# Decode-attention backward on one core: five of 128 stores cut into pieces on two queues instead of one

## The chip, the cores and the metric

The kernel runs on one NeuronCore of a Trainium2 chip. The metric is the device time of one execution in microseconds (us). The engines are named as the profile names them: PE (TensorE, matrix multiply), DVE (VectorE), ACT (ScalarE), POOL (GpSimd) and SP (SyncE, which only issues transfers here). PEld is the weight load of PE. Three engines issue DMA transfers, each on a queue of its own: SP on q1, ACT on q10, POOL on q0. The transfers of all three are carried by the same 16 DMA engines of the core.

## The reference

The kernel computes softmax attention for a single query row and its gradients, for 64 heads (2 batches of 32), 8192 keys, head dimension 128, all in bf16:

```
scores = q . k^T / sqrt(128);  p = softmax(scores);  out = p . v
inputs:  q, grad_out [2,32,1,128];  k, v [2,32,8192,128]
returns: out, dq [2,32,1,128];  dk, dv [2,32,8192,128]
```

With one query row, `dv` of a head is the outer product of `p` with `grad_out`, and `dk` that of the scores' gradient with `q`. So each head reads 2 MB of keys and 2 MB of values, and writes 2 MB of `dk` and 2 MB of `dv`: 512 MB (of 2^20 bytes) in all, which is 537 of the 539 MB (of 10^6 bytes) on the profile's page.

## The kernel before, in words

**Tiling.** The keys of a head are one tile `kt` of 128 partitions x 16 KB: partition p holds tokens 64p to 64p+63, one contiguous row of 16 KB in memory. The values are a tile `vt` of the same shape. There are five buffers of each (`UNITS = 5`). Per head, PE turns the tile blockwise (line 115), ACT copies the result out of PSUM (line 122), PE forms scores and products, DVE finishes the softmax, and DVE overwrites `vt` with `dv` and `kt` with `dk` in place (`outer`, line 288). From there the tiles are stored.

**Order.** The work is written out by hand, with no reordering within an engine (`manual_schedule`, lines 377 to 443). The loop runs over heads h = 0 to 64, in eight steps j. Step j of turn h turns an eighth of head h and finishes head p = h - 1. In step 3 of turn h the `dv` of head p is stored, in step 7 its `dk`; they are called value store p and key store p below. At the end of turn h, SP issues `load(h + 3)`: first the keys, then the values. A load needs a free buffer: the keys of head p + 5 normally wait for key store p to land, the values of p + 5 for value store p (SP, line 106). SP and ACT both go through their instructions strictly in order; so does POOL.

**Landing semaphores.** A transfer that is issued raises a semaphore when it has landed. The program has eight of them for the transfers of SP and ACT together, and eight more for POOL's. They are dealt out in turn, along one order of all transfers which the planner (the Tile layer) makes when the kernel is built. An instruction that is to issue a transfer first waits until the transfer that had the same semaphore before has landed. The planner's order around a head p, read off the semaphore numbers of the program: keys p + 4, values p + 4, value store p, key store p, and so on.

**The stores.** `store(h, w)` (line 345) sends a tile off as a single transfer from ACT (line 348), 128 rows of 16 KB, for 123 of the 128 tiles; the last head's two tiles go in halves. The five tiles with `(2h + w) % 26 == 12` go through `store_by_fifteen` (line 306) instead. These are the `dv` tiles of heads 6, 19, 32, 45 and 58. There POOL sends a tile off in 24 transfers (`rows`, line 316), made of every fourth row, or of two rows 32 apart. Between these stand 11 transfers `turn(n)` (line 302): each copies 2n pieces of 4 bytes into the tile `spare`, whose contents nobody reads. Each row of a `rows` transfer of size 8192 moves as two pieces of 8 KB, one of size 16384 in one piece. Rows 16 to 19 and 48 to 51 (`fifth`), eight of 128, are sent two at a time and by themselves.

Of the kernel before, what the change touches and what calls it, by code (L numbers as in the profile page):

```python
# [18 lines left out]
RARE = 26  # L19
# [4 lines left out]
def kernel(  # L24
# [11 lines left out]
    nc = tc.nc  # L36
# [40 lines left out]
    dk_v = out_2.rearrange("b h (p n) d -> (b h) p n d", n=NT)  # L77
    dv_v = out_3.rearrange("b h (p n) d -> (b h) p n d", n=NT)
# [17 lines left out]
    heads = [Head() for _ in range(BH)]  # L96
# [200 lines left out]
    def turn(n):  # L297

        i = 4 * len(turns)
        turns.append(n)  # L300
        two = lambda t: t.rearrange("p (a b) -> p a b", a=2)
        nc.gpsimd.dma_start(  # L302
            out=two(spare[0:n, :])[:, :, i : i + 2], in_=two(q_rows[0:n, :])[:, :, 0:2]
        )

    def store_by_fifteen(h, w):

        dst, src = (dv_v, dk_v)[w][h], heads[h].kv[1 - w]

        def rows(lo, n, step=4, size=8192):
            own = slice(lo, lo + step * (n - 1) + 1, step)
            nc.gpsimd.dma_start(out=dst[own], in_=src[own], max_dma_last_dim=size)  # L316

        def fifth(r):
            rows(16 + r, 2, step=32)

        for r in range(4):

            if r == 1:
                fifth(r)
                turn(14)
            rows(52 + r, 11)
            rows(r, 4, size=16384)
            if r == 0:
                fifth(r)
                turn(3)  # L330
            elif r == 3:
                turn(10)
                fifth(r)
                turn(9)
            else:
                turn(5)
            rows(20 + r, 3)
            if r == 2:
                fifth(r)
                turn(14)  # L340
            rows(96 + r, 8)
            rows(32 + r, 4, size=16384)
            turn(5)

    def store(h, w, a=0, b=NT):
        if (2 * h + w) % RARE == RARE // 2 - 1:
            return store_by_fifteen(h, w)
        nc.scalar.dma_start(out=(dv_v, dk_v)[w][h][:, a:b, :], in_=heads[h].kv[1 - w][:, a:b, :])
# [16 lines left out]
    for i in range(2):  # L365
# [3 lines left out]
            out=qz[i][:, 0 : 4 * BH].rearrange("p (h z) -> p h z", z=4)[:, :, 3], in_=tps[:]  # L369
# [7 lines left out]
    with tc.manual_schedule():  # L377
# [59 lines left out]
        for w, dst in enumerate((o_rows, dq_rows)):  # L437
            tps = ps_tp.tile([BH, P], BF16, name="tps", tag="tp")
            nc.tensor.transpose(tps[:], colsT[:, w, :], ident_bf[:])  # L439
            rows = const.tile([BH, D], BF16, name=f"rows{w}")  # L440
# [33 lines left out]
```

## Time and profile before

| | us |
|---|---|
| median of 3 runs | 1276.52 (1276.35 to 1276.57) |
| the profiled execution | 1276.51 |
| its span, first to last instruction | 1274.4 |

| engine | busy us | share of the span |
|---|---|---|
| PE | 1060.1 | 83% |
| DVE | 892.3 | 70% |
| ACT | 961.0 | 75% |
| POOL | 104.5 | 8% |

The page also has rows for DMA: the mean busy share of the 16 DMA engines and the bytes per second in 40 slices of the span, the share of each queue, and for each kind of issue the median time from issue to landing: 21.4 us for a load of keys, 30.6 us for one of values, 24.9 and 22.5 us for stores from ACT. The first piece of each of the five tiles is issued at 138.63, 389.08, 648.81, 905.30 and 1164.06 us.

How to read it: a timeline row gives start, length, engine, line, operation, `out<-in`, and in brackets how long the engine sat idle before and what ended that. A letter q behind an engine's name means its sequencer: it issues or waits, and the engine computes nothing. Each turn of the loop issues two loads (SP, line 106) and two stores (ACT, line 348).

### The profile page before, as it was taken

How to read it: one execution, taken by the hardware profiler on the slowest of the kernel's cores; microseconds unless marked ns; L12 is line 12 of the kernel's file. 1: busy time of each engine (PE TensorE's matmuls, PEld its weight loads, DVE VectorE, ACT ScalarE, POOL GpSimd, SP SyncE). 2: the span in 40 equal slices, each digit the busy share in tenths (PEclk: the TensorE clock that was granted, in tenths of full speed). 3: DMA queues.
4: the chain of work that ended last, by engine and by line, in shares of the span. 5: the costliest groups of instructions: out<-in, count | busy, mean ns of one | idle time of the engine just before them, and what ended most of it. 6: DMA issues, size and time to landing. Idle time of an engine off the chain costs nothing. (4 is left out here: it accounts for less than half of the span.)

```text
span 1274.4 us, 31597 instructions
## 1 busy us (share of the span) xinstructions
PE 1060.1 (83%) x13444; PEld 708.9 (56%) x13444; DVE 892.3 (70%) x1576; ACT 961.0 (75%) x1107; POOL 104.5 (8%) x189
## 2 busy tenths in 40 slices
PE   5999889849998798399996984999969849999694
PEld 4666566526665565266664652666546526666462
DVE  1888858728887487288884863888856738888486
ACT  5888778739887687289875873988848838888583
POOL 1000211000002110000021200000212000001220
PEclk9999989969999799699997996999989979999797
DMA  9999999999999999999999999999999999999998
GB/s 394 419 429 426 428 426 427 426 431 429 427 428 426 425 426 427 426 422 427 428 426 423 424 426 425 422 426 429 425 418 427 428 428 415 429 427 428 424 425 345
DMA packets 43837, 539.00 MB, mean 423 GB/s; under 512 B 10192, under 2 KB 10192, under 8 KB 10192
## 3 DMA queue, kind: packets, MB, share of 16 engines
q1 hardware_dynamic: 18432, 268.44, 49.7%
q10 hardware_dynamic: 18320, 258.02, 47.7%
q0 software_dynamic: 6944, 10.51, 2.2%
q8 instruction: 105, 1.72, 0.5%
q14 instruction: 36, 0.29, 0.1%
HBM read 268.47 MB, written 268.47 MB: 421 GB/s over the span
## 5 line engine op out<-in xcount | busy, mean ns | idle before, releaser
L122 ACT CAST ev<-tp 128x1024 bf16<-128x1024 f32 x960 | 933.3, 1017 | 290.0 <-PE tp L115 141.2
L115 PE MATMUL tp<-ident_bf,vt 128*128 128x128 bf16 x4096 | 328.9, 226 | 132.3 <-ACT ev L122 117.2
L115 PEld LDWEIGHTS <-vt 128*128 128x128 bf16 x4096 | 266.7, 102 | 210.3 <-issue 185.0
L115 PE MATMUL tp<-ident_bf,kt 128*128 128x128 bf16 x4096 | 318.7, 221 | 8.8 <-DMA kt<-in_k_dram 7.2
L115 PEld LDWEIGHTS <-kt 128*128 128x128 bf16 x4096 | 238.9, 98 | 135.7 <-issue 124.5
L288 DVE TENSOR_TENSOR vt<-qd,P 128x2048 bf16<-128x2048 bf16 x256 | 306.6, 1219 | 0.2 <-DVE rawsb L142 0.2
L288 DVE TENSOR_TENSOR kt<-qd,dS 128x2048 bf16<-128x2048 bf16 x256 | 306.1, 1217 | 0.0
L131 PE MATMUL raw<-ev,qz 128*4 128x512 bf16 x2048 | 202.3, 384 | 0.3 <-ACT ev L122 0.3
L142 DVE COPY rawsb<-raw 128x512 f32<-128x512 f32 x128 | 88.6, 692 | 132.9 <-PE raw L131 130.5
L316 POOL DMA_DIRECT2D out_dram<-vt x120 | 67.0, 560 | 1018.5 <-DVE vt L288 822.4
L174 DVE TENSOR_REDUCE mp<-turned 128x1 f32<-128x64 f32 x64 | 14.1, 221 | 131.0 <-PE turned L148 130.2
L256 PE MATMUL acc<-vt,wz 128*32 128x512 bf16 x1024 | 102.1, 389 | 0.0
L256 PE MATMUL acc<-kt,wz 128*32 128x512 bf16 x1024 | 100.9, 387 | 0.9 <-DVE wz L203 0.9
L148 PE MATMUL turned<-ident_f,rawsb 128*128 128x128 f32 x512 | 87.4, 296 | 11.6 <-DVE rawsb L142 9.8
L120 DVE CAST ev<-tp 128x1024 bf16<-128x1024 f32 x64 | 78.4, 1225 | 16.7 <-PE tp L115 16.7
L131 PEld LDWEIGHTS <-qz 128*4 128x4 bf16 x2048 | 46.5, 81 | 55.3 <-issue 3.9
L148 PEld LDWEIGHTS turned<-ident_f,rawsb 128*128 128x128 f32 x512 | 57.1, 147 | 29.5 <-DVE rawsb L142 29.3
L256 PEld LDWEIGHTS <-wz 128*32 128x32 bf16 x2048 | 52.4, 93 | 29.2 <-DVE wz L203 1.6
L180 DVE TENSOR_REDUCE gm<-misc 1x1 f32<-1x128 f32 x64 | 17.8, 279 | 45.2 <-PE misc L178 45.2
L200 PEld LDWEIGHTS misc<-ld,ones_f 128*128 128x128 f32 x256 | 38.4, 189 | 15.3 <-DVE ld L227 15.3
L200 PE MATMUL misc<-ld,ones_f 128*128 128x1 f32 x256 | 45.9, 248 | 0.7 <-DVE ld L227 0.6
L302 POOL DMA_DIRECT2D spare<-in_q_dram x57 | 34.2, 600 | 123.0 <-DMA out_dram<-vt 107.8
(45 smaller groups left out, 332.7 us busy)
## 6 DMA issues: line engine op xcount, KB each, us to landing
kt<-in_k_dram SPq DMA_DIRECT2D x64, 2048.0 KB, 21.4
vt<-in_v_dram SPq DMA_DIRECT2D x64, 2048.0 KB, 30.6
out_dram<-kt ACTq DMA_DIRECT2D x63, 2048.0 KB, 24.9
out_dram<-vt ACTq DMA_DIRECT2D x58, 2048.0 KB, 22.5
out_dram<-vt POOLq DMA_DIRECT2D x20, 176.0 KB, 22.6
out_dram<-vt POOLq DMA_DIRECT2D x40, 64.0 KB, 22.8
out_dram<-vt POOLq DMA_DIRECT2D x20, 128.0 KB, 22.5
out_dram<-vt ACTq DMA_DIRECT2D x2, 1024.0 KB, 8.6
```

Source lines behind the costliest of these rows:

```text
L115: nc.tensor.matmul(tp[:, i, :], lhsT=x.kv[w][:, n, :], rhs=ident_bf[:], start=True, stop=True)
L120: nc.vector.tensor_copy(out=ev[:], in_=tp[:])
L122: nc.scalar.copy(out=ev[:], in_=tp[:])
L131: nc.tensor.matmul(raw[32 * k : 32 * k + 4, :], lhsT=qz[w][:, at : at + 4], rhs=evs[k // 2][:, 4 * (k % 2) : 4 * (k % 2) + 4, :].rearrange ...
L142: nc.vector.tensor_copy(out=x.raw[:], in_=raw[:])
L148: nc.tensor.transpose(out[:, i], x.raw[:, i * P : (i + 1) * P], ident_f[:])
L180: nc.vector.reduce_max(out=x.gm[:], in_=mT, axis=AX.X)
L200: nc.tensor.matmul(x.lsum, lhsT=ones_f[:], rhs=x.ld[:, w : w + 1], start=True, stop=True)
L256: nc.tensor.matmul(acc[32 * g : 32 * g + 32, :], lhsT=wz[w][:, n // 4, at : at + 32], rhs=rows[:, n : n + 4, :].rearrange("p n d -> p (n d)"),
L288: nc.vector.tensor_tensor(out=x.kv[1 - w][:, n : n + CH, :].rearrange("p n (d t) -> p n d t", t=2), in0=row.unsqueeze(1).to_broadcast([P, ...
L302: nc.gpsimd.dma_start(out=two(spare[0:n, :])[:, :, i : i + 2], in_=two(q_rows[0:n, :])[:, :, 0:2])
L316: nc.gpsimd.dma_start(out=dst[own], in_=src[own], max_dma_last_dim=size)
```

## The change

`store_by_fifteen` alone is changed. ACT now sends eight transfers of four rows each at its start: rows lo, lo + 4, lo + 8, lo + 12 for lo = 0 to 3 and 32 to 35. They stand in ACT's instruction stream where, for any other tile, the one store stands. POOL sends the other 96 rows: 20 + r, three rows, and 96 + r, eight rows, for r = 0 to 3; rows 16 to 19 as one transfer and rows 48 to 51 as another; and rows 52 to 95 as one transfer of 44 rows. That makes 11 transfers of POOL's with rows, and 9 turns (7 for the second and the fourth of the five tiles, where `odd` is 1) instead of 24 and 11. Over the five stores POOL's transfers go from 175 to 96, and ACT gets 40 more. All rows of POOL's move as two pieces of 8 KB; ACT's rows are not cut.

```
+        odd = ((2 * h + w) // RARE) % 2
-        def rows(lo, n, step=4, size=8192):
+        def rows(lo, n, step=4):
             own = slice(lo, lo + step * (n - 1) + 1, step)
-            nc.gpsimd.dma_start(out=dst[own], in_=src[own], max_dma_last_dim=size)
-
-        def fifth(r):
-            rows(16 + r, 2, step=32)
-
+            nc.gpsimd.dma_start(out=dst[own], in_=src[own], max_dma_last_dim=8192)
+
+        for lo in (0, 1, 2, 3, 32, 33, 34, 35):
+            nc.scalar.dma_start(out=dst[lo : lo + 13 : 4], in_=src[lo : lo + 13 : 4])
         for r in range(4):
-            if r == 1:
-                fifth(r)
-                turn(14)
-            rows(52 + r, 11)
-            rows(r, 4, size=16384)
+            if r == 2 and odd:
+                rows(48, 4, 1)
+                turn(12)
+            rows(20 + r, 3)
             if r == 0:
-                fifth(r)
-                turn(3)
-            elif r == 3:
-                turn(10)
-                fifth(r)
-                turn(9)
-            else:
-                turn(5)
-            rows(20 + r, 3)
-            if r == 2:
-                fifth(r)
-                turn(14)
+                if odd:
+                    rows(16, 4, 1)
+                    turn(12)
+                else:
+                    turn(4)
+                    rows(16, 4, 1)
+                    turn(8)
+            if r == 2 and not odd:
+                turn(8)
+                rows(48, 4, 1)
+                turn(4)
             rows(96 + r, 8)
-            rows(32 + r, 4, size=16384)
             turn(5)
+        rows(52, 44, 1)
+        turn(5)
```

## The prediction

> **What bounds the kernel now.** I read the DMA rows of the page first, then SP's waits, then the timelines of POOL and ACT around one of the five stores, then stages by window.
>
> ```profile
> DMA  9999999999999999999999999999999999999998
> GB/s 394 419 429 426 428 426 427 426 431 429 427 428 426 425 426 427 426 422 427 428 426 423 424 426 425 422 426 429 425 418 427 428 428 415 429 427 428 424 425 345
> ...
> q1 hardware_dynamic: 18432, 268.44, 49.7%
> q10 hardware_dynamic: 18320, 258.02, 47.7%
> q0 software_dynamic: 6944, 10.51, 2.2%
> ```
>
> The 16 DMA engines are busy in every slice at some 427 GB/s, while PE is busy 83% and ACT 75%. So bytes are the bound: what the DMA engines lose is lost, and what a compute engine loses can be made up. The loads, q1, take 49.7% of 16 x 1274.4 us for 128 transfers: 10134 / 16 / 128 = 4.95 us for one 2 MB transfer that has all engines to itself, twice that beside a store.
>
> ```profile
> SPq L106 <- DMA out_dram<-kt: 906.1, 59, 39.0
> SPq L106 <- DMA out_dram<-vt: 206.3, 21, 11.4
> ```
>
> SP's queue stands still nearly all the time until a store lands. So the loads are as far ahead as the five buffers let them be: when stores stop being issued, loads stop as soon as the buffers are full.
>
> ```profile
> 138.63 1.67 POOL L316 DMA_DIRECT2D out_dram<-vt  x3 [133.92 <-DVE vt L288]
> 140.30 0.58 POOL L302 DMA_DIRECT2D spare<-in_q_dram  x1
> 140.88 1.68 POOL L316 DMA_DIRECT2D out_dram<-vt  x3
> 142.55 0.62 POOL L302 DMA_DIRECT2D spare<-in_q_dram  x1
> 147.37 0.56 POOL L316 DMA_DIRECT2D out_dram<-vt  x1 [4.20 <-DMA out_dram<-vt]
> 149.20 0.57 POOL L302 DMA_DIRECT2D spare<-in_q_dram  x1 [1.27 <-DMA out_dram<-vt]
> ```
>
> This is a store by pieces: eight transfers back to back, then the ninth waits 4.20 us for the first to land, and so on. That is what eight landing semaphores dealt in turn look like. POOL does nothing else, so its wait costs nothing. ACT has other work, and the same rule. SP's timeline, the load's time to landing among the DMA issues, and ACT's timeline:
>
> ```profile
> 397.93 0.33 SPq L106 DMA_DIRECT2D kt<-in_k_dram  x1
> ```
>
> ```profile
> kt<-in_k_dram SPq DMA_DIRECT2D x1, 2048.0 KB, 20.5
> ```
>
> ```profile
> 403.31 3.90 ACT L122 CAST ev<-tp 128x1024 bf16<-128x1024 f32 x4 [0.56 <-PE tp L115]
> 418.54 0.34 ACTq L348 DMA_DIRECT2D out_dram<-vt  x1
> 418.97 1.93 ACT L122 CAST ev<-tp 128x1024 bf16<-128x1024 f32 x2 [11.77 <-issue]
> ```
>
> Here value store 20 is the eighth transfer after the load of keys 22 (issued 397.93, landed 20.5 us later, at 418.4). ACT stands from 407.2 until 418.5, issues, and only then copies on: 11.77 us idle, with PE behind it. A store of ACT's thus waits for a load of SP's that shares its semaphore. In the stage around it the DMA engines stay full:
>
> ```profile
> core 0: us, PE busy (x) PEld busy (x) DVE busy (x) ACT busy (x) POOL busy (x), PEclk, DMA share, GB/s
> ...
> 400.00:418.00 18.00, 8.39 (x114) 5.22 (x111) 10.12 (x15) 6.53 (x7) 3.87 (x7) 0.81 1.01 427
> ...
> 1205.00:1240.00 35.00, 33.57 (x440) 22.29 (x437) 29.50 (x53) 31.39 (x37) 6.79 (x13) 1.00 1.01 424
> 1240.00:1252.00 12.00, 11.33 (x153) 7.43 (x149) 10.73 (x18) 10.35 (x14) 2.46 (x5) 1.00 0.94 395
> ```
>
> The two columns that matter are ACT busy and, last but one, DMA share (1.01: full). So a short stop of ACT is free. The 1205 to 1240 row shows compute at its own pace (PE 96% busy): ACT issues stores at 1202.54, 1210.91, 1219.02, 1227.39, 1235.49, 1243.84 and 1251.96, 8.24 us apart or 16.5 us a head. DMA needs 4 x 4.95 = 19.8 us a head.
>
> **The change, part by part.** The sum is made against the profiled execution, 1276.51 us (span 1274.4 and 2.1 around it); the median, 1276.52, is the same.
>
> *Fewer transfers of POOL's.* q0's 2.2% is 449 engine-us; its 10.51 MB at q1's price (10134 engine-us for 268.44 MB) are 397. The other 52, 3.3 us per DMA engine, are turns and landing marks of 177 transfers. 79 go: -1.5 us. Ends: 0 and -3.3. POOL's issue time (0.56 us each) hides behind its waits.
>
> *Other places for eight rows, one transfer of 44 rows.* No view tells which DMA engine carries a row. Bounds: the engines are full until 1240 and 0.94 busy to 1252, so a better balance can give 0.06 x 12 = 0.7 us; one row more per store on one engine costs 5 x 4.95 / 8 = 3 us. I take 0, having no row for either side.
>
> *Eight issues on ACT.* 8 x 0.34 us instead of no issue: 2.7 us of ACT per store, hidden in waits like the 11.77 us one. Without that cover it would be 13.6 us over five stores.
>
> *What these eight wait for.* Eight transfers in a row take all eight landing semaphores, so each of the last eight transfers of SP and ACT in the planner's order must have landed before ACT goes on. In that order value store p follows the loads of keys and values p + 4; the pieces stand in its place. So the eighth piece waits for values p + 4. Behind it on ACT are the copies out of PSUM, so PE (two buffers) and then DVE stop too, and key store p, which frees the buffer that keys p + 5 need. Keys and values p + 4 need stores p - 1, already issued. So ACT waits for the last loads that can be issued at all, until all five buffers are full and q10 is empty. Queued behind key store p are SP's loads of p + 5. POOL's pieces do not wait for ACT.
>
> Followed through the second store (p = 19, all up to 389.1 as before): value store 18 lands at 372.48 + 35.5 = 408.0, key store 18 at 380.61 + 37.7 = 418.3; then q10 is empty. Keys 22 land at 418.4. Values 22 (before: 398.36 + 30.7 = 429.1, beside stores) now need 4.95 alone: 423.4. Keys 23 (issued 418.41 on the landing of key store 18): 428.3. Values 23: 433.3. ACT stands from 389.1 to 433.3, 44 us. Key store 19 comes one half-head later, 8.2, and its first packet about 1 us after the issue (an estimate: SP's first load is issued at 0.74, and the trace's first packet of its queue starts at 1.74): 442.5. So 9.2 us without load or store. Key store 19 then runs alone, and keys 24 follow its landing another 1.1 us late. From there each store sets off a load, 9.9 us of DMA for every 8.24 of compute: full again. Hole: 10.3 us, less what is left of POOL's pieces, of which the last is the 44-row transfer: eight pieces of 8 KB for each of 11 engines, at 4.95 / 16 = 0.31 us each, 2.5 us. I take 8 us a store. Ends: 4 (much more of POOL's work left over) and 11 (none, and a later key store). The 44 us themselves compute makes up in 13 heads: 13 x (19.8 - 16.5) = 43.
>
> The first, third and fourth store have the same order of loads: 4 x 8 = 32 us (16 to 44).
>
> *The fifth store* has only five heads behind it. Without shift: key store 57 lands at 1155.59 + 35.0 = 1190.6, keys 61 at 1170.70 + 21.1 = 1191.8; values 61, keys 62, values 62 alone: 3 x 4.95, so 1206.6. Key store 58 at 1214.8, key store 62 four heads (65.9) later: 1280.7, against 1251.96 now. What follows is 12.8 us to the last key store's issue (1264.79) as now, and its landing, 8.0 us now behind three halves in the queue, 4 to 5 alone. So the end comes 28.7 - 3.5 = 25 us later (20 to 28).
>
> Sum: 1276.5 - 1.5 + 0 + 32 + 25 = 1332. From the ends: 1276.5 - 3.3 - 0.7 + 16 + 20 = 1308.5 and 1276.5 + 3 + 44 + 28 = 1351.5; not all at once, so 1311 to 1347.
>
> **The rivals.**
>
> *Keys, not values.* If the planner puts the values' load behind the first piece, where POOL's first piece now stands in its order, the last wait is for keys p + 4. Then values p + 4, 4.95 us, fill half of the hole: 3 us a store, and the end 20 us late: 1276.5 - 1.5 + 12 + 20 = 1307 (1296 to 1315). Against it: a store of ACT's is placed behind the copies of its step, later than POOL's piece.
>
> *No hole; not slower.* ScalarE's wait is hidden like the one at 407. It decides at 9.2 us before the loads run out: were ACT free by 433.3 - 9.2 = 424.1, after 35 us, no gap would open, as loads fill q1 and compute is faster than DMA. That is so if the pieces meet semaphores of transfers landed long ago. Then only the -1.5 us are left, 1275 (1272.5 to 1276.5). For it: DMA share 1.01 through the 11.77 us. Against it: one shared semaphore made that wait, and eight pieces share all. The Trainium skill, DMA: Bandwidth & Descriptors, section Issuing engines are not separate DMA queues, says that the choice of the issuing engine saves only the sequencer's issue time, because all transfers run on the same 16 engines. By that rule this rival's 1275 would hold; the 11.77 us row shows a cost of issuing from ACT that the rule does not have.
>
> *The change does not place rows as it means to.* If the 44 rows went to four engines, 11 each instead of 4, and nothing waited, seven rows too many per store: 5 x 7 x 0.62 = 22 us, 1297. The profile has nothing for it.
>
> **How the numbers follow.** Forecast 0.64, keys case 0.13, no hole 0.17, rows misplaced 0.02, more than 1347 0.04. Predicted: 1332 us. The range reaches down over the keys case, 1296, and up to 1347; it leaves out 0.17 and 0.03. The likeliest case alone: 1311 to 1347. Within 0.2%, 2.6 us, is about what a measurement of this kernel can tell from no change. No hole splits into 0.10 within and 0.07 faster (fewer marks and a better balance, 1.5 + 0.7 + some of the 1.8 left of the 3.3); the rest, 0.83, is slower.
>
> **What would show it.** Right: after the first piece at about 389 ACT idle some 44 us, with its eight issues strewn over it; DMA share well under 1 for some 8 us behind it, five times; q0's share near 2.0%; compute-paced stores from 1237 on. Wrong: ACT's eight issues within 3 us, or DMA at 1.01 through the wait; the keys case if values p + 4 still run when ACT goes on.

## The result, and the profile after

The changed kernel takes 1380.32 us (median of 6 runs, 1379.60 to 1382.76) against 1276.55 us of the kernel before beside it (6 runs): a ratio of 1.0811, 95% interval 1.0799 to 1.0822, 103.8 us slower. The forecast was 1332 us, in a range of 1296 to 1347. The profiled execution took 1382.76 us; its span is 1380.9 us, 106.5 more than before.

The page after, the slices of the span and the queues:

```profile
DMA  9999969999999599999995999999959999999686
GB/s 398 418 428 427 401 234 424 426 428 427 429 429 377 231 425 428 426 429 428 428 380 224 427 427 428 429 429 427 380 221 421 427 429 427 430 427 376 234 343 288
...
q1 hardware_dynamic: 18432, 268.44, 46.7%
q10 hardware_dynamic: 18640, 260.65, 44.5%
q0 software_dynamic: 4496, 7.88, 1.7%
```

Where every slice was full before, five now stand out, at 221 to 234 GB/s, and the last two are thin as well. The DMA engines moved the same 539 MB; they had nothing to move in between.

ACT's timeline around the first of the five tiles:

```profile
138.58 41.15 ACTq L317 DMA_DIRECT2D out_dram<-vt  x8
179.82 1.93 ACT L122 CAST ev<-tp 128x1024 bf16<-128x1024 f32 x2 [40.30 <-DMA vt<-in_v_dram]
...
188.14 0.34 ACTq L343 DMA_DIRECT2D out_dram<-kt  x1
```

The eight issues of line 317 are spread over 41.15 us, and ACT copies nothing for 40.30 us; what ended the wait is a load of values. One by one the eight go out at 138.58, 140.25, 159.79, 166.62, 167.26, 167.89, 171.78 and 179.13 us (the same view in narrow windows). In the planner's order their semaphores belonged to value store 4, key store 4, keys 9, values 9, value store 5, key store 5, keys 10 and values 10: the long stops are those of the four pieces that share with a load. Over the five tiles ACT waits 237.1 us for loads of values, 50.5 at most. Key store 6 is issued 8.3 us after ACT goes on. SP's timeline beside it:

```profile
140.36 0.33 SPq L106 DMA_DIRECT2D kt<-in_k_dram  x1
140.79 0.45 SPq L106 DMA_DIRECT2D vt<-in_v_dram  x1
162.32 0.33 SPq L106 DMA_DIRECT2D kt<-in_k_dram  x1
162.75 0.39 SPq L106 DMA_DIRECT2D vt<-in_v_dram  x1
195.79 0.33 SPq L106 DMA_DIRECT2D kt<-in_k_dram  x1
196.58 0.33 SPq L106 DMA_DIRECT2D vt<-in_v_dram  x1
```

The loads issued at 140 are those of head 9, those at 162.3 those of head 10, p + 4. The next go out at 195.79, 7.7 us after key store 6. And the stages (the last two columns are the DMA share and GB/s):

```profile
core 0: us, PE busy (x) PEld busy (x) DVE busy (x) ACT busy (x) POOL busy (x), PEclk, DMA share, GB/s
138.00:160.00 22.00, 2.68 (x39) 1.51 (x37) 4.51 (x5) 1.52 (x2) 6.88 (x12) 0.63 1.01 418
160.00:170.00 10.00, 0.00 (x0) 0.00 (x0) 0.00 (x0) 0.00 (x0) 3.42 (x6) 0.50 0.95 366
170.00:180.00 10.00, 0.00 (x0) 0.00 (x0) 0.00 (x0) 0.17 (x1) 1.22 (x2) 0.50 0.81 306
180.00:190.00 10.00, 8.68 (x97) 6.42 (x96) 3.55 (x9) 7.93 (x11) 0.00 (x0) 0.77 0.15 61
190.00:200.00 10.00, 9.65 (x131) 6.11 (x124) 9.78 (x15) 9.28 (x10) 0.00 (x0) 1.00 0.72 259
200.00:210.00 10.00, 9.79 (x125) 7.28 (x123) 6.97 (x17) 8.72 (x12) 0.00 (x0) 1.00 0.96 401
```

First compute stands (PE 0.00) while the DMA engines work on; then compute runs while they stand (0.15). Against a share of 1.01 the rows from 160 to 210 miss 0.6 + 2.0 + 8.6 + 2.9 + 0.5 = 14.6 us of all DMA engines.

### The profile page after: what moved, and what is told of

Its sections match the earlier page's. It is cut to its first block, busy times and chain, and to the rows that moved or that the text cites. A ratio compares the mean times of both kernels' runs of the same rounds, so it can differ in the third digit from the quotient of the medians.

```text
span 1380.9 us, 31601 instructions
## 1 busy us (share of the span) xinstructions
PE 1052.0 (76%) x13444; PEld 705.3 (51%) x13444; DVE 893.6 (65%) x1576; ACT 958.8 (69%) x1107; POOL 59.6 (4%) x110
## 3 DMA queue, kind: packets, MB, share of 16 engines
q0 software_dynamic: 4496, 7.88, 1.7%
## 5 line engine op out<-in xcount | busy, mean ns | idle before, releaser
L122 ACT CAST ev<-tp 128x1024 bf16<-128x1024 f32 x960 | 931.6, 1018 | 401.2 <-DMA vt<-in_v_dram 237.1
L115 PE MATMUL tp<-ident_bf,vt 128*128 128x128 bf16 x4096 | 323.1, 223 | 225.4 <-ACT ev L122 225.4
L115 PEld LDWEIGHTS <-vt 128*128 128x128 bf16 x4096 | 262.6, 101 | 302.3 <-issue 296.2
L314 POOL DMA_DIRECT2D out_dram<-vt x55 | 31.6, 576 | 1147.8 <-DVE vt L288 1090.2
L160 PE MATMUL pb<-nat,ident_bf 64*128 64x256 bf16 x64 | 10.2, 282 | 52.8 <-ACT ev L122 52.7
L180 DVE TENSOR_REDUCE gm<-misc 1x1 f32<-1x128 f32 x64 | 17.8, 279 | 43.2 <-PE misc L178 43.2
```

Of the source, the lines that this page charges most:

```text
L115: nc.tensor.matmul(tp[:, i, :], lhsT=x.kv[w][:, n, :], rhs=ident_bf[:], start=True, stop=True)
L122: nc.scalar.copy(out=ev[:], in_=tp[:])
L180: nc.vector.reduce_max(out=x.gm[:], in_=mT, axis=AX.X)
```

## The experiments

Each ran beside the kernel before on the same chip as itself, with two runs, except the first (eleven) and the one with two pieces on ACT (eight). Four theories were told apart: 1, ACT stands for landing semaphores that its eight transfers share with SP's loads; 2, POOL's new layout is slow; 3, transfers of four rows from ACT's queue are slow in themselves; 4, every transfer from ACT costs the same.

### The eight given back to POOL

```
-        def rows(lo, n, step=4):
+        def rows(lo, n, step=4, size=8192):
...
-            nc.gpsimd.dma_start(out=dst[own], in_=src[own], max_dma_last_dim=8192)
+            nc.gpsimd.dma_start(out=dst[own], in_=src[own], max_dma_last_dim=size)
...
         for lo in (0, 1, 2, 3, 32, 33, 34, 35):
-            nc.scalar.dma_start(out=dst[lo : lo + 13 : 4], in_=src[lo : lo + 13 : 4])
+            rows(lo, 4, size=16384)
```

> The changed kernel with its eight ACT transfers given back to POOL, as eight uncut transfers of the same four rows ahead of its others; ACT issues nothing for these five tiles, as before. Theory 1 (the loss is ScalarE standing for landing semaphores): the loss is gone, 1274 to 1277 us, at best 1.5 us under the kernel before for the marks that fewer transfers save. Theory 2 (the loss is in POOL's new layout, the 44-row transfer on a few DMA engines): the loss stays, 1350 us or more. Theory 3 (transfers of four rows from ACT's queue are slow in themselves): as theory 1.

Measured: 1277.51 us against 1276.64, ratio 1.0009 (1.0000 to 1.0018). That is 0.5 us above the expected range, and 0 to 2.3 us slower than before. The loss is gone, so theory 2 falls. From its page:

```profile
DMA  9999999999999999999999999999999999999997
...
q0 software_dynamic: 5776, 10.51, 2.3%
```

The 5776 packets are 1168 fewer than before, yet the queue's share is 2.3% where it was 2.2%. The packets in the two traces say why. Those under 512 bytes, marks and turns, took 42.1 engine-us instead of 52.6; but the 960 pieces of 8 KB took 339 ns on average instead of 313, as 43 of them took over 400 ns (11 before). Together with a small rest the queue took 15 engine-us more, 0.9 us for each of the 16 engines. Why those pieces are slower in the new layout is open.

### The eight alone, in the kernel before

```
+        for lo in (0, 1, 2, 3, 32, 33, 34, 35):
+            nc.scalar.dma_start(out=dst[lo : lo + 13 : 4], in_=src[lo : lo + 13 : 4])
         for r in range(4):
...
             rows(52 + r, 11)
-            rows(r, 4, size=16384)
...
             rows(96 + r, 8)
-            rows(32 + r, 4, size=16384)
```

> The kernel before with only its eight four-row transfers of POOL's moved to eight of ACT's; the eleven-row transfers, the rows two at a time and all turns stay as before. Theory 1: the eight take all eight landing semaphores as in the changed kernel, so 1365 to 1395 us, ACT idle 40 to 50 us at each of the five tiles. Theory 2: 1274 to 1290 us. Theory 3: as theory 1.

Measured: 1374.14 us, ratio 1.0762 (1.0742 to 1.0782): 97.5 of the 103.8 us come with this part by itself. ACT stands 37.98 us at the first tile (40 to 50 were expected) and up to 47.3 later.

### Eight tiny transfers, in the kernel before

```
+    tiny = []
...
+        for _ in range(8):
+            i = 2 * len(tiny)
+            tiny.append(i)
+            nc.scalar.dma_start(out=spare2[:, i : i + 2], in_=q_rows[0:4, 0:2])
         for r in range(4):
...
+    spare2 = const.tile([4, 128], BF16)
```

> The kernel before, whole, plus eight transfers of four pieces of 4 bytes from ACT at the start of each of the five stores by pieces, into a spare tile. Next to no data is moved, but they take the same eight semaphores. Theory 1: ACT waits for the load of values p + 4 as in the changed kernel, and the time is 1360 to 1395 us. Theories 2 and 3: 1277 to 1285 us, eight issues of about 0.4 us on ACT.

Measured: 1367.24 us, ratio 1.0708 (1.0688 to 1.0727). Eight times sixteen bytes per tile cost 90.6 us. ACT's timeline:

```profile
137.67 0.53 ACTq L325 DMA_DIRECT2D spare<-in_q_dram  x1
137.67 1.02 ACT L122 CAST ev<-tp 128x1024 bf16<-128x1024 f32 x1
141.05 36.47 ACTq L325 DMA_DIRECT2D spare<-in_q_dram  x7
177.62 1.93 ACT L122 CAST ev<-tp 128x1024 bf16<-128x1024 f32 x2 [38.93 <-DMA vt<-in_v_dram]
```

The same wait for the same load, with next to nothing to carry. Theory 3 falls: neither the rows nor their places matter for the bulk of the loss, only that ACT issues eight transfers in a row.

### The eight issued by SP

```
-            nc.scalar.dma_start(out=dst[lo : lo + 13 : 4], in_=src[lo : lo + 13 : 4])
+            nc.sync.dma_start(out=dst[lo : lo + 13 : 4], in_=src[lo : lo + 13 : 4])
```

> The changed kernel with the eight transfers issued by SP instead of ACT, at the same place of the program. The transfers are the same four rows on a hardware queue; SP waits for the semaphores instead, and holds back only its own next loads. Theory 1: most of the loss gone; the last piece now meets the landing of key store p, so the loads of p + 4 may go some 10 us late while stores run: 1275 to 1310 us. Theory 3: the loss stays, 1350 us or more. Theory 2: the loss stays.

Measured: 1294.20 us, ratio 1.0136 (1.0117 to 1.0154). Most of the loss goes when the engine that waits has nothing else to do. What stays fits the delay of the loads that was expected, seen in SP's timeline at the first tile; that this delay makes all of the 17.6 us was not tested:

```profile
143.49 27.68 SPq L317 DMA_DIRECT2D out_dram<-vt  x8
171.28 1.23 SPq L106 DMA_DIRECT2D kt<-in_k_dram  x1
177.21 0.33 SPq L106 DMA_DIRECT2D vt<-in_v_dram  x1
```

The eight take SP 27.68 us, and the keys of head 10, issued at 161.18 in the kernel before, go out at 171.28.

### Two, six and seven of the eight on ACT

The changed kernel with the first n places of the list left on ACT and the rest given to POOL, uncut, through `rows` with its parameter `size` as above; for n = 6:

```
-        for lo in (0, 1, 2, 3, 32, 33, 34, 35):
-            nc.scalar.dma_start(out=dst[lo : lo + 13 : 4], in_=src[lo : lo + 13 : 4])
+        for lo in (0, 1, 2, 3, 32, 33):
+            nc.scalar.dma_start(out=dst[lo : lo + 13 : 4], in_=src[lo : lo + 13 : 4])
+        for lo in (34, 35):
+            rows(lo, 4, size=16384)
```

> The changed kernel with two of its eight four-row transfers left on ACT, the other six given to POOL, uncut. Theory 1 (which semaphore the last piece meets): piece n of ACT waits for the transfer nine minus n places ahead of the first piece in the planner's order; the second for key store p - 2, landed some 9 us after the first piece is ready. That wait is covered: 1275 to 1282 us. Theory 4 (every transfer from ACT costs the same, 104 us / 40 = 2.6 us): 1276.6 + 5 x 2 x 2.6 = 1303 us.

> Six of the eight on ACT. Theory 1: the longest wait is that for values p + 3 or key store p - 1, not for the loads of p + 4; by the changed kernel's second store ACT goes on some 12 us earlier than with eight (443.2 against 455.1), which closes most of the hole: 2 to 5 us for each of the first four stores, 15 to 25 for the last: 1297 to 1325 us. Theory 4: 1276.6 + 5 x 6 x 2.6 = 1355 us.

> Seven of the eight on ACT. Theory 1: the last piece waits for the keys p + 4, about 5 us before their values: some 5 us less per store than the changed kernel, 4 x 14 + 31 = 87 us: 1350 to 1370 us. Theory 4: 1276.6 + 5 x 7 x 2.6 = 1368 us. This run alone does not tell the two apart; with two and six it does.

| on ACT | us | against before | interval of the ratio | ACT copies on at, first tile |
|---|---|---|---|---|
| 0 | 1277.51 | +0.9 | 1.0000 to 1.0018 | - |
| 2 | 1279.59 | +2.7 | 1.0000 to 1.0032 | - |
| 6 | 1321.68 | +44.8 | 1.0319 to 1.0379 | 167.41 |
| 7 | 1344.75 | +67.8 | 1.0499 to 1.0560 | 173.73 |
| 8 | 1380.32 | +103.8 | 1.0799 to 1.0822 | 179.82 |

Not a price per transfer (theory 4: 1303 and 1355 us for two and six): two are all but free, the seventh costs 23 us and the eighth 36. Six at the first tile:

```profile
137.54 29.78 ACTq L317 DMA_DIRECT2D out_dram<-vt  x6
167.41 1.93 ACT L122 CAST ev<-tp 128x1024 bf16<-128x1024 f32 x2 [28.93 <-DMA out_dram<-vt]
```

The name in the bracket is inferred. One by one, the fourth of the six, on the semaphore of values 9, goes out at 165.45, the fifth and sixth without a stop behind it, at 166.09 and 166.72: the long waits are for the loads of head 9, as theory 1 has it. With seven, the seventh goes out at 173.04, on the semaphore of keys 10. With six, ACT copies on 12.4 us earlier than with eight, and the loss over five tiles is 59 us smaller, 11.8 a tile: what comes off the end of the wait comes off the time nearly one for one. With two and six the time lies in the range that theory 1 gave; with seven the expectation of 1350 us and more was some 5 us too high.

### One tile alone in the new form

```
-            return store_by_fifteen(h, w)
+            return (store_by_fifteen_new if h == 6 else store_by_fifteen)(h, w)
```

and the same with `h == 58`; `store_by_fifteen` is the old function there, `store_by_fifteen_new` the changed one.

> The new form for the first of the five tiles alone (head 6), the old form for the other four. In the changed kernel everything up to this store is as before, and its second store starts 17.8 us late. Theory 1 with the loss of one store being what the DMA engines stand still, 14.3 us in that kernel's first hole, and loads that run slower alone: 1291 to 1297 us, all of it kept to the end. The prediction's term, 8 us: 1283 to 1286. If compute or DMA made the loss up later: 1277 to 1280.

> The new form for the last of the five tiles alone (head 58), the old form for the other four. Theory 1: the last store has too few heads behind it for compute to make its wait up, so it costs more than the others: in the changed kernel the first piece comes 70.1 us late at head 58 and the end 106.5 late, so 36 us: 1305 to 1318 us. If each of the five cost the same, 104 / 5 = 21: 1297 us. The prediction's term for it was 25 us: 1301.

Measured: 1294.38 us for the first tile alone, ratio 1.0136 (1.0090 to 1.0182), 17.8 us more than before (by the interval 11.5 to 23.2); 1305.55 us for the last alone, 1.0223 (1.0193 to 1.0253), 28.6 us more (24.6 to 32.3). What the first tile loses is not made up in the 57 heads behind it. The terms add up to nearly the whole: 4 x 17.8 + 28.6 = 99.8, of 103.8; turned round, (103.8 - 28.6) / 4 = 18.8 us for one of the first four. In the run with the last tile alone ACT goes as follows:

```profile
1162.65 45.38 ACTq L317 DMA_DIRECT2D out_dram<-vt  x8
1208.13 1.93 ACT L122 CAST ev<-tp 128x1024 bf16<-128x1024 f32 x2 [44.54 <-DMA vt<-in_v_dram]
1216.74 0.34 ACTq L382 DMA_DIRECT2D out_dram<-kt  x1
...
1283.47 0.34 ACTq L382 DMA_DIRECT2D out_dram<-kt  x1
```

## Why the prediction was wrong, and where it was right

**Right: direction and mechanism.** The eight pieces take all eight landing semaphores, the last waits for the values p + 4, and ACT holds back key store p until all five buffers are full. ACT stands 47.6 us at the second tile, which the forecast followed through with 44, 40.3 at the first and 50.5 at most. The timeline, the tiny transfers and the row of 2, 6, 7 and 8 pieces each show a part of it; the planner's order was as the prediction read it (values p + 4 ahead of the pieces, not behind the first). The Trainium skill (DMA: Bandwidth & Descriptors, Issuing engines are not separate DMA queues) says that starting transfers from several engines at once saves only the sequencer's time of starting them. It speaks of what is saved, not of what the engine waits for first, and here that decides: the same eight transfers cost 0.9 us from POOL, 17.6 from SP and 103.8 from ACT, and eight tiny ones from ACT 90.6. "No hole" is what two transfers give, not eight.

**Right: the last tile.** Forecast with no shift: ACT on at 1206.6, key stores 58 and 62 at 1214.8 and 1280.7, 25 us. Measured with that tile alone: 1208.1, 1216.7, 1283.5, and 28.6 us, just above the forecast's end of 28, with an interval that holds the 25 as well.

**Wrong: "I take 8 us a store. Ends: 4 and 11."** The step that failed is the size of the hole at one of the first four stores: it costs 17.8 us, above the upper end of 11 (though by its interval only just), and 18.8 by the whole kernel. Four times the difference is 39 of the 48 us by which 1332 missed. By the rows of the first tile, the parts of that term:

| part | forecast, us | measured, us |
|---|---|---|
| DMA idle before ACT goes on (160 to 180) | 0 | 2.6 |
| from there to key store p (180 to 190) | 9.2 - 2.3 | 8.6 |
| behind key store p (190 to 210) | 1.1 | 3.4 |
| busy but slower | 0 | 3.4 |
| sum | 8.0 | 18.0 |

The first line: the forecast let the engines work at full share until ACT goes on. About 0.6 us are lost around 162, as the loads already issued run out before SP can issue the last pair at 162.3, when key store 5 has landed. The other 2.0 are lost at the end, where the engines run out one after another (a share of 0.88 from 174 to 176, 0.33 from 178 to 180); the last packet of values 10 ends at 178.5, the eighth piece goes out at 179.13, and ACT copies on at 179.82.

The second: POOL's pieces were to fill 2.3 us of the hole. But while ACT stood they had only loads beside them and were nearly done when it went on: POOL's last issue is at 172.14, its last packet ends at 180.9. On how many DMA engines the 44 rows lay, no run shows.

The third: key store 6 needs 7.7 us from its issue to the next load, where 4.95 and about a microsecond were reckoned. It starts at the full rate (1.01 and 421 GB/s from 189 to 192), but then the engines run out one after another (0.65 from 192 to 195): its packets run from 189.0 to 195.3, the load is issued at 195.79, and the load's first packet starts at 196.7.

The fourth was not in the sum at all: the loads of the wait were priced at the full rate. From 160 to 180 the engines were busy for 17.6 us and moved 6.72 MB, 382 GB/s of busy time, against 423 (427 / 1.01) in full stages; over 138 to 210 that is 3.4 us of work at the full rate. The packets in the trace agree: over the whole kernel those of the loads add up to 10326 engine-us where they were 10135, and POOL's pieces of 8 KB took 369 ns on average instead of 313, which makes 2.4 and 0.7 us for each tile and engine. Why they are slower is open. That no store runs beside them is not the reason by itself: from 5 to 37 us of the kernel before, with no store issued yet, loads moved 428 and 424 GB/s at shares of 1.01 and 1.00.

The list was followed for one store only. The other 9 us (48 - 39) are the last tile's 3.6, the 1.5 that was not gained (below), and 4 by which the five tiles cost more together than apart (103.8 - 99.8), which is within the interval of the 17.8.

**Wrong: fewer marks, -1.5 us, and other places for the rows, 0.** With the eight given back to POOL the time is +0.9 us (0 to 2.3): no gain. That run takes away only 39 of the 79 transfers. In the changed kernel, by the packets of its trace, POOL's marks and turns took 31.5 engine-us instead of 52.6 and ACT's 1.3 more, so 1.2 us per engine were saved, near the forecast. What was mis-sized is the term taken as 0: pieces of 8 KB are dearer in the new layout, 339 and 369 ns against 313, which outweighs the saving. The forecast's ends for both terms together, -4.0 to +3, hold the +0.9.

**Smaller slips.** An issue of four rows takes ACT 0.60 us (median of the 40), not 0.34, so 4.8 us a tile; nearly all of it lies inside the wait. And the sign "q0's share near 2.0%" overlooked that a quarter of the rows leave POOL: it is 1.7%, for 7.88 MB instead of 10.51.

## What to carry to other kernels

Count the landing semaphores before cutting a transfer up on a compute engine's queue: as many pieces in a row as there are semaphores make that engine wait for every transfer in flight that shares them, here another queue's loads included. Put such pieces on a queue whose engine has nothing else to do, and see what stands behind them there. When a wait is covered by work in flight, follow that work to its end: here it ran out only because the waiting engine was the one that had to issue more.

## What the runs showed that was not expected

The same tiny transfers that move 128 bytes a tile cost 7% of the kernel. And a DMA engine counted as busy is not always as fast: 306 GB/s at a share of 0.81 (378 per share) at the end of the wait, 259 at 0.72 (360) when transfers start again after the hole, 427 at 1.01 (423) in full stages. By the packets of the trace it is the loads: a row of 16 KB of a load took 710 ns on average from 163 to 180 and 895 from 195.7 to 200, against 613 in the kernel before (130 to 250), while a row from ACT took 611 to 626 in the same stretches.
